# A retention layer and a snake MLP on one core: q and k of the first tiles read in rows of eight tokens, group 0 in another order, first states summed in 64x64 tiles

## The chip, the core and the metric

The kernel runs on one core of a Trainium2 chip. The metric is the device time of one execution in microseconds; the lower the better. Five engines work side by side, each through a queue of its own that it takes in order: TensorE (PE in the profile, its weight loads PEld), VectorE (DVE), ScalarE (ACT), GpSimd (POOL) and SyncE (SP). In this kernel POOL's queue also issues nearly all reads from memory.

## The reference, cut to what matters

```python
# q, k, v: float32 [4 batches, 8 heads, 768 tokens, 64]
gamma = 1.0 - 2.0 ** (-5.0 - np.arange(H))
for t in range(S):
    state = gamma * state + einsum('bhd,bhe->bhde', k[:, :, t], v[:, :, t])
    y[:, :, t] = einsum('bhd,bhde->bhe', q[:, :, t], state) / sqrt(64)
x = y.transpose(0, 2, 1, 3).reshape(3072, 512)
h = x @ w_in                        # w_in 512 x 2048
s = np.sin(alpha * h)
g = h + s * s / (alpha + 1e-9)
out = g @ w_out                     # w_out 2048 x 512, out 3072 x 512 float32
```

## The kernel before

**Tiles.** Tokens are cut into chunks of 128: six in each of the four batches, 24 in all. `order` takes the first chunk of each batch first (called e0 to e3), then the others batch by batch; P is the same list, so P4 is the fifth tile. The tiles form groups of 4, 2, 2, 2, 2, 2, 2, 2, 2 and 4. The MLP runs group by group.

**Attention of a tile.** The recurrence is worked out chunk by chunk: q and k are transposed (`half_T` for e0 to e3, `stage_T` for P4 to P7, a transposing DMA from the SP queue in `turn` for the rest), scores are multiplied out (`stage_A`, later `scores`), masked and weighted with powers of gamma on VectorE into aT, and multiplied with v (`stage_M`, later `round_of` and `mix`). A first chunk has no earlier state. For all later ones a `burst` runs on TensorE: the state times q (`inter`), the next tile's scores, the mix with v, and the update of the state (`sums`, or inside `round_of`). VectorE then writes x (`leave`, run as "exit"), adds the state (`keep`), and another engine rounds it (`hand`). v is scaled with powers of gamma (`scale_v`) before it enters a state.

**The states of first chunks.** When a burst ends one batch, its state sums are those of the next batch's first chunk (`now` is then not `old`). They are eight matmuls with all 128 tokens as the contracted dimension, behind the mix.

**The MLP.** A `Slot` multiplies x with 128 columns of w_in for each f that it covers, takes the sine on ScalarE, squares it on ScalarE ("A") or VectorE ("D"), and on VectorE adds it to h (`add`, L496). `ff_out` multiplies one f of one tile with w_out (128x512, called a piece here), 16 pieces for a tile. From group 1 on, `phase` interleaves the slots of a group with the pieces of the group before it and with the bursts at fixed places.

**Group 0** is written out by hand. While reads arrive, TensorE runs fillers (`idle_work`). The first three tiles' x is made as their reads land, slots 0 to 3 (called a, b, c, d) run on those three tiles alone, e3 is worked in between, its columns of slots 0 to 3 are made up in one further slot (t here), and slots 4 to 15 run on all four tiles. The pieces of tiles 0, 1 and in part 2 follow the slots; 13 of the 26 pieces left for tiles 2 and 3 (`fill`) run before phase 1.

**Memory.** `load_chunk` reads one chunk of q, k or v through POOL's queue and turns float32 into bf16: token by token, so 256 bytes are read and 128 written at a time, 1024 packets for 128 KB. Weights come in pieces of 256 and 512 KB. q and k of e0 come through SP as float32. Eight counters serve POOL's reads in turn, so a read waits until the eighth read before it has landed.

**PSUM.** There are four single banks (tag "mm"), and two pairs ("two", "pa").

Of the kernel before, what the change touches and what calls it, by code (L numbers as in the profile page):

```python
# [16 lines left out]
def kernel(  # L17
# [32 lines left out]
    sizes = [4]+[2]*8+[4]  # L50
# [34 lines left out]

    def load_chunk(j, names="qkv"):
        for name, src in (("q", q), ("k", k), ("v", v)):
            if name not in names:
                continue
            if name == "v":  # L90
                t = big.tile([128, H, D], BF16, name="vr", tag="vr", bufs=11)
            else:
                if ("qk", j) not in raw:
                    raw["qk", j] = big.tile([128, 2, H, D], BF16, name="qkr", tag="qkr", bufs=9)
                t = raw["qk", j][:, "qk".index(name)]
# [67 lines left out]
    tok = consts.tile([128, NCH, 2], F32, name="tok")  # L163
    for b in range(2):
        nc.gpsimd.iota(tok[64 * b:64 * b + 64], pattern=[[C, NCH], [64, 2]], channel_multiplier=1, base=0,
                       allow_small_or_imprecise_dtypes=True)
    load_chunk(order[3], "qk")
    for h in range(2):
        load_w_out(0, h)
# [19 lines left out]
    for h in range(H):  # L189
        nc.scalar.activation(out=dec[:, h % 2, h // 2, :], in_=tio, func=ACTF.Exp, scale=lng[h], bias=back[:, h:h + 1])  # L190
# [16 lines left out]

    def later_tables():
        for b in range(2):
            for p in range(NP):  # L210
                nc.vector.memset(lgq[64 * b:64 * b + 64, p:p + 1], lng[head(b, p // 2, p % 2)])
# [32 lines left out]
    def half_T(j, i, eng, bank=None):  # L244

        if i == 0:
            st["qkT", j] = work.tile([128, 2 * NP, 128], BF16, name="qkT", tag="qkT", bufs=6)
        pt = psum.tile([128, NP, 128], BF16, name="pt", tag="mm", bufs=4) if bank is None else bank.rearrange("i (p t) -> i p t", p=NP)
        for p in range(NP):
            nc.tensor.transpose(pt[:, p, :], raw["qk"[i], j][:, 2 * p:2 * p + 2, :].rearrange("p h d -> p (h d)"), ident)  # L250
        o = st["qkT", j][:, i * NP:(i + 1) * NP, :]
        if eng is nc.scalar:
# [23 lines left out]
    def stage_A(j):  # L276
        qkT = st["qkT", j]
        pa = psum.tile([128, 2, NP, 128], F32, name="pa", tag="pa")
        for p in range(NP):
# [4 lines left out]
        aT = work.tile([128, 2, NP, 128], BF16, name="aT", tag="aT", bufs=2)  # L284
        m = dec.rearrange("p e n t -> p (e n) t") if j % NCH == 0 else mask_bc
        nc.vector.tensor_mul(aT.rearrange("p e n t -> p (e n) t"), pa.rearrange("p e n t -> p (e n) t"), m)
        st["aT", j] = aT
# [18 lines left out]
    def stage_M(j, bank):  # L306
# [3 lines left out]
        for p in range(NP):  # L310
            for e in range(2):
                nc.tensor.matmul(py[half(e), p, :], vs[:, 2 * p + e, :], aT[:, e, p, :],
                                 start=(p == 0), stop=True, skip_group_check=True)
        nc.scalar.copy(x_of(j), py)
# [49 lines left out]
    def sums(now, to, lo):  # L364

        ks, vs = raw["k", now], raw["v", now]
        for f in range(2 if wide(now) else 1):
            for b, m, e in heads:
                h = head(b, m, e)
                nc.tensor.matmul(to[b][half(e), lo + 64 * m:lo + 64 + 64 * m],  # L370
                                 ks[half(b), f, 2 * m + e, :] if wide(now) else ks[:, h, :],
                                 vs[half(b), f, 2 * m + e, :] if wide(now) else vs[:, h, :],
                                 start=False, stop=True, skip_group_check=True)
# [436 lines left out]
```

## Time and profile before

| | |
|---|---|
| median of 3 runs | 210.59 us (210.5 to 211.37) |
| the profiled execution | 210.93 us, its span 209.1 us |
| instructions | 5702 |
| PE busy, matmul instructions | 199.3 us, 2327 |
| DVE, ACT busy | 151.9 us each |
| POOL busy, issuing of reads among it | 116.5 us |
| TensorE clock granted | 1.00 throughout |
| queue of POOL's reads | 79248 packets, 13.38 MB |
| chain that ended last | PE 77%, DMA 13%, POOL 6% |

The profile is of one execution. In the timeline the columns are start and duration in us, engine, line, operation, output and inputs, shapes, count; in brackets the idle time before it and what ended it. In the table of windows each engine's busy time is followed by the granted clock, the DMA share and GB/s. In the groups, the two numbers behind the first bar are busy us in all and mean ns of one.

### The profile page before, as it was taken

Reading aid. Unit: us, or ns where it says so; the run is one execution under the profiler, and the core shown is the slowest. Engines: PE = TensorE matmul, PEld = TensorE weight load, DVE = VectorE, ACT = ScalarE, POOL = GpSimd, SP = SyncE. Lnnn points to the kernel's source line nnn. Section 1 sums busy time; section 2 is a strip of 40 time slices with the busy share of each in tenths; the row PEclk is TensorE's granted clock in tenths of the full one; section 3 lists DMA queues with packets and bytes.
Section 4 is the critical chain, followed back from the end, with each engine's and each line's share of the span. In section 5 each row is a group of like instructions: output and inputs, shape, how many; then the busy total and the mean of one; then the engine's idle time right before and its main releaser. Section 6 shows DMA issues by size and latency. Waiting matters only on the chain.

```text
span 209.1 us, 5702 instructions
## 1 busy us (share of the span) xinstructions
PE 199.3 (95%) x2327; PEld 123.6 (59%) x2354; DVE 151.9 (73%) x310; ACT 151.9 (73%) x309; POOL 116.5 (56%) x157
## 2 busy tenths in 40 slices
PE   7898999999999999999999999999999999999994
PEld 2444544457776766766666766766767654444453
DVE  4788788877989968768868768867788965656220
ACT  7777687557998787787787787786785779999001
POOL 8999948599999999999599911002022200000000
PEclk9999999999999999999999999999999999999999
DMA  9999999999999999999999995412412101010212
GB/s 130 149 170 194 202 200 184 151 161 198 161 126 142 79 167 183 182 100 180 143 173 159 145 176 54 103 57 47 102 54 52 50 5 50 2 50 3 100 50 100
DMA packets 102026, 24.76 MB, mean 118 GB/s; under 512 B 93024, under 2 KB 99056, under 8 KB 102000
## 3 DMA queue, kind: packets, MB, share of 16 engines
q0 software_dynamic: 79248, 13.38, 87.9%
q1 hardware_dynamic: 22608, 10.96, 26.0%
q8 instruction: 18, 0.29, 0.6%
q14 instruction: 8, 0.07, 0.1%
q10 hardware_dynamic: 144, 0.07, 0.1%
HBM read 27.27 MB, written 6.29 MB: 160 GB/s over the span
## 4 chain that ended last, share of the span: by engine, by line
PE 77%; DMA 13%; POOL 6%; issue 2%; DVE 0%; POOLq 0%; DVEq 0%
PE po L506 34%; PE ph L481 33%; DMA qkr<-in_k_dram 5%; DMA w_out<-in_moe_w_out_dram 5%; DMA w_in<-in_moe_w_in_dram 3%; PE py L336 2%; POOL qg L229 2%; PE poh L531 2%; POOL qkr L100 2%; PE py L386 1%; POOL vr L100 1%; POOL w_in L131 1%; PE pa L346 1%; PE py L395 1%; PE pt L264 1%
## 5 line engine op out<-in xcount | busy, mean ns | idle before, releaser
L496 DVE SCALAR_TENSOR_TENSOR gT<-s,rec_alpha,ph 128x256 bf16<-128x256 f32 (+3 forms) x164 | 79.9, 523 | 32.8 <-ACT s L489 32.5
L481 PE MATMUL ph<-xT,w_in 128*128 128x256 bf16 (+3 forms) x652 | 98.1, 290 | 0.3
L484 ACT ACTIVATE s<-ph,alpha_sb 128x256 f32<-128x256 f32 (+3 forms) x164 | 76.2, 507 | 30.3 <-PE ph L481 30.2
L506 PE MATMUL po<-w_out,gT 128*128 128x512 bf16 x346 | 91.3, 379 | 3.1 <-issue 2.7
L481 PEld LDWEIGHTS <-w_in 128*128 128x128 bf16 x656 | 63.3, 98 | 33.8 <-issue 1.1
L489 ACT ACTIVATE s<-s 128x512 f32<-128x512 f32 (+1 forms) x91 | 57.0, 627 | 2.9
L506 PEld LDWEIGHTS <-gT 128*128 128x128 bf16 x368 | 33.9, 98 | 29.5
L452 POOL CAST s_q<-s_f 128x256 bf16<-128x256 f32 x5 | 2.0, 397 | 35.0 <-DVE s_f L448 18.0
L518 DVE COPY o_sb<-po 128x512 f32<-128x512 f32 x20 | 13.8, 691 | 9.8 <-PE po L506 9.8
L120 POOL DMA_DIRECT2D qk_seq<-in_q_dram x24 | 17.0, 766 | 2.7 <-DMA v_seq<-in_v_dram 2.6
L120 POOL DMA_DIRECT2D qk_seq<-in_k_dram x24 | 16.8, 716 | 0.8 <-issue 0.4
L120 POOL DMA_DIRECT2D v_seq<-in_v_dram x24 | 16.9, 765 | 0.0
L156 POOL TENSOR_TENSOR v_seq<-v_seq,kgq 128x512 bf16<-128x512 bf16 x13 | 13.5, 1057 | 4.6 <-DMA v_seq<-in_v_dram 4.6
L433 DVE TENSOR_TENSOR xT<-py,qg 128x512 bf16<-128x512 f32 x19 | 13.0, 685 | 0.8 <-PE py L402 0.8
L361 DVE TENSOR_TENSOR aTw<-pa,maskq 128x768 bf16<-128x768 f32 x13 | 12.4, 954 | 0.0
L100 POOL DMA_DIRECT2D vr<-in_v_dram x11 | 10.2, 927 | 1.2 <-DMA w_in<-in_moe_w_in_dram 1.1
L551 PE MATMUL spare<-warm 128*128 128x512 bf16 x24 | 8.4, 480 | 1.2 <-DVE warm L176 1.2
L535 ACT COPY o_sb<-poh 128x256 f32<-128x256 f32 (+1 forms) x2 | 0.6, 320 | 11.7 <-PE poh L531 11.2
L349 DVE TENSOR_TENSOR aT<-pa,mask 128x1024 bf16<-128x1024 f32 x7 | 8.5, 1218 | 0.0
L452 ACT CAST s_q<-s_f 128x256 bf16<-128x256 f32 x14 | 5.5, 393 | 3.1 <-DVE s_f L446 2.7
L100 POOL DMA_DIRECT2D qkr<-in_k_dram x7 | 6.3, 896 | 1.7 <-DMA w_out<-in_moe_w_out_dram 1.7
L100 POOL DMA_DIRECT2D qkr<-in_q_dram x7 | 6.4, 910 | 0.9 <-DMA w_in<-in_moe_w_in_dram 0.9
(99 smaller groups left out, 160.8 us busy)
## 6 DMA issues: line engine op xcount, KB each, us to landing
out_dram<-o_sb SPq DMA_DIRECT2D x23, 256.0 KB, 2.6
w_in<-in_moe_w_in_dram POOLq DMA_DIRECT2D x6, 256.0 KB, 10.3
w_out<-in_moe_w_out_dram POOLq DMA_DIRECT2D x3, 512.0 KB, 11.2
vr<-in_v_dram POOLq DMA_DIRECT2D x11, 128.0 KB, 5.5
qk_seq<-in_q_dram POOLq DMA_DIRECT2D x16, 80.0 KB, 7.1
qk_seq<-in_k_dram POOLq DMA_DIRECT2D x16, 80.0 KB, 5.2
v_seq<-in_v_dram POOLq DMA_DIRECT2D x16, 80.0 KB, 5.3
qkr<-in_q_dram POOLq DMA_DIRECT2D x7, 128.0 KB, 6.8
```

Source lines behind the costliest of these rows:

```text
L100: nc.gpsimd.dma_start(out=t, in_=chunk_of(src, j))
L120: nc.gpsimd.dma_start(out=o, in_=src[bt, head(b, m, e), cs[0] * C:, :].rearrange("(f i) d -> i f d", i=64))
L156: eng.tensor_mul(t, t, by[:, j % NCH, :, None].to_broadcast([128, H, D]))
L349: return {"mask": lambda: nc.vector.tensor_mul(aT.rearrange("p e n t -> p (e n) t"), pa.rearrange("p e (n t) -> p (e n) t", n=NP), mask_bc)}
L361: return {"mask": lambda: nc.vector.tensor_mul(aT, pa[:, :, 0:384].rearrange("p e (m t) -> p e m t", m=2), maskq[:, None, None, :].to_broa ...
L433: nc.vector.tensor_mul(o, st["pyw", old][:, :, 0:256].rearrange("p b (m t) -> p b m t", m=2), by)
L481: nc.tensor.matmul(self.ph[:, m, :], w_in[:, i, f * 128:(f + 1) * 128], xT[g][:, i, self.lo:self.hi], start=(m == 0 and i == 0), stop=(i = ...
L484: nc.scalar.activation(out=self.s[:, m, :], in_=self.ph[:, m, :], func=ACTF.Sin, scale=alpha_sb[:, f:f + 1])
L489: nc.scalar.activation(out=self.s, in_=self.s, func=ACTF.Square)
L496: nc.vector.scalar_tensor_tensor(gT[self.g][:, f, self.lo:self.hi], self.s[:, m, :], rec_alpha[:, f:f + 1], self.ph[:, m, :], op0=ALU.mult ...
L506: nc.tensor.matmul(po[g, ts], gT[g][:, f, ts * C:(ts + 1) * C], w_out[:, f, :], start=(f == 0), stop=(f == FF - 1))
L518: nc.vector.tensor_copy(o_sb, po[g, ts])
```

## The change

- **Rows.** q of e1, e2, e3 and k of e2, e3 are read as 128 rows (16 for each head) of eight tokens: 2 KB read and 1 KB written at a time. Partition p then holds eight neighbouring tokens of one head. `half_T` turns such a tile with sixteen 64x64 transposes, and the copy out of PSUM puts the tokens back in order. k of e1 goes to a tile of its own; the tag of the other q and k has seven buffers instead of nine.
- **k back.** The states of e2 and e3 need k by token. `back_k` turns it back from its transposed form, in two bursts each (old = P10, P11 and P15, P16), with a copy on VectorE.
- **First states.** `sums` works in 64x64 tiles for both cases; the two halves of the tokens go to columns of their own, which `keep` adds up. It now runs ahead of the scores. In the last burst half of the mix runs ahead of the wait for `inter`.
- **Group 0** has another order: the reads, the fillers, the masks apart from the scores (`mask_A`), x of e1 and e2 copied by VectorE, the transposes of e3 ahead of slot a, first tables on other engines (`tok` on VectorE), `later_mask` in phase 2, and the slots, squares, sums and pieces listed one by one. The transposes of e0 and e1 read one head each (64 columns).

```diff
+    def rows_of(t, j):
+        b, c = divmod(j, NCH)
+        return t[b, :, c * C:(c + 1) * C, :].rearrange("h (i f) d -> h i (f d)", f=8)
+    def load_rows(j, name):
+        src = q if name == "q" else k
+        t = raw[name, j] = big.tile([128, 8, D], BF16, name=f"{name}f", tag=f"{name}f", bufs=3 if name == "q" else 2)
+        nc.gpsimd.dma_start(out=t.rearrange("p f d -> p (f d)"), in_=rows_of(src, j))
+    def by_rows(j, name):
+        return name == "q" and j in order[1:4] or name == "k" and j in order[2:4]
...
-    load_chunk(0, "v")
-    load_chunk(order[1])
-    load_chunk(order[2])
-    for h in range(2):
-        load_w_in(0, h)
...
-    load_chunk(order[3], "qk")
-    for h in range(2):
-        load_w_out(0, h)
+    load_chunk(order[1], "k")
+    load_chunk(order[3], "k")
+    load_chunk(order[1], "q")
+    load_chunk(order[2], "k")
+    load_chunk(order[2], "q")
+    load_chunk(order[1], "v")
+    load_chunk(order[0], "v")
+    load_w_in(0, 0)
+    load_chunk(order[2], "v")
+    load_chunk(order[3], "q")
+    load_w_out(0, 0)
+    load_w_in(0, 1)
+    load_w_out(0, 1)
     load_chunk(order[3], "v")
     load_w_in(1)
     load_w_out(1)
...
+        if by_rows(j, "qk"[i]):
+            for f in range(8):
+                for x in range(2):
+                    nc.tensor.transpose(pt.rearrange("i p t -> i (p t)")[half(x), 64 * f:64 * f + 64],
+                                        raw["qk"[i], j][half(x), f, :], ident[half(x), half(x)])
+            o = o.rearrange("d m (i f) -> d m i f", f=8)
+            pt = pt.rearrange("d p t -> d (p t)").rearrange("d (f m i) -> d m i f", f=8, m=NP)
...
+    def back_k(j, x):
+        if x == 0:
+            raw["k", j] = big.tile([128, 2, NP, D], BF16, name="kn", tag="kf", bufs=2)
+        pt = psum.tile([128, NP, D], BF16, name="pt", tag="mm", bufs=4)
+        for m in range(NP):
+            for f in range(2):
+                nc.tensor.transpose(pt[half(f), m, :], st["kT", j][half(x), m, half(f)], ident[half(x), half(x)])
+        nc.vector.tensor_copy(raw["k", j][:, x], pt)
...
     def sums(now, to, lo):
-        for f in range(2 if wide(now) else 1):
+        for r in range(2):
             for b, m, e in heads:
...
+                    h, f = head(b, m, e), b ^ r
+                    bank, at, vh = f, lo + 128 * r, vs[half(f), h, :]
+                    kh = ks[half(f), h // NP, h % NP, :] if now in order[2:4] else ks[half(f), h, :]
+                last = nc.tensor.matmul(to[bank][half(e), at + 64 * m:at + 64 * m + 64], kh, vh,
+                                        start=False, stop=True, skip_group_check=True)
...
     def burst(old, new, first=None, apart=False):
...
+        elif now is not None and now is not old:
+            last = sums(now, st["py", old], 256)
         more = scores(new) if new is not None else {}
+        if old in P[10:12] + P[15:17]:
+            back_k(e2 if old in P[10:12] else e3, (P.index(old) - 10) % 5)
...
         if wide(old):
-            mix(old)
-            if now is not None and now is not old:
-                sums(now, py, 256)
+            mix(old, rest)
...
+    # group 0, around the first three tiles and slot a
+    stage_A(e0)
+    half_T(e1, 0, nc.scalar)
+    half_T(e1, 1, nc.scalar)
+    idle_work(4)
+    later_tables()
+    stage_A(e1)
+    mask_A(e0)
+    mask_A(e1)
+    half_T(e2, 0, nc.vector)
+    half_T(e2, 1, nc.scalar)
+    stage_M(e1, front[:, 0], nc.vector)
+    stage_A(e2)
+    stage_M(e0, front[:, 0])
+    mask_A(e2)
...
+    stage_M(e2, front[:, 0], nc.vector)
+    half_T(e3, 0, nc.vector)
+    half_T(e3, 1, nc.scalar)
+    slot("a", 0, 0, n3, 1, "mm")
+    scale_v(e2, nc.vector)
+    slot("b", 1, 0, n3, 1, "mm")
+    stage_A(e3)
+    sl["b"].sq("A")
+    sl["a"].sq("D")
+    slot("c", 2, 0, n3, 1, "mm")
+    slot("d", 3, 0, n3, 1, "mm")
+    sl["a"].add()
...
+    mask_A(e3)
+    sl["c"].add()
+    stage_M(e3, pye(), nc.vector)
+    pairs(2)
+    scale_v(e3, nc.vector)
+    ff_out(0, 2, 2)
+    scale_v(e0, nc.vector)
+    scale_v(e1, nc.vector)
+    slot("t", 0, n3, n4, 4, "pa")
+    sl["t"].sq("A")
+    slot("4", 4, 0, n4, 1, "mm")
+    sl["d"].add()
```

`pairs(f)` is the piece f of tiles 0 and 1. `slot(name, ...)` makes a `Slot` under a name.

More of the change, by code (lines that the diff above doesn't have):

```diff
@@ L639 @@
     P = order
[L640 to L650 removed]
+    n2, n3, n4 = 2 * C, 3 * C, 4 * C
+    e0, e1, e2, e3 = order[:B]
     outs = out_pieces(0, (2, 3))[6:]
+    sl, more = {}, {}
     def fill(n):
@@ L695, with slot, pairs @@
-    scale_v(P[4], nc.gpsimd)
-    m4 = scores(P[4])["mask"]
-    F((0, 1), (13,))
-    fill(1)
-    stage_T(P[5], nc.scalar, "mm")
-    a.add()
-    m4()
-    fill(4)
-    scale_v(P[5], nc.vector)
-    fresh = burst(P[4], P[5], apart=True)
-    run(fresh, "keep", "hand", "mask")
-    F((0, 1), (14,))
-    F((0, 1), (15,))
-    run(fresh, "exit")
+    def slot(name, f, lo, hi, nf=1, tag="mm"):
+        sl[name] = Slot(0, f, (lo, hi), nf, tag)
+    def pairs(f):
+        if f == 0:
+            both = psum.tile([128, 2, d_model], F32, name="po", tag="two")
+            po[0, 0], po[0, 1] = both[:, 0], both[:, 1]
+        for t in range(2):
+            ff_out(0, t, f)
@@ L711 @@
+    fill(1)
+    pairs(14)
+    upto(burst(P[4], P[5], apart=True))
     load_chunk(P[7])
```

347 lines of the change are left out of this document (206 added, 141 removed).

## The prediction

> **What bounds the kernel now.** I read the page's busy shares first, then the chain that ended last, then the timeline from 0 to 50 us, the windows with their DMA rates, the groups by form, and one stretch of the late phases.
>
> ```profile
> PE 199.3 (95%) x2327; PEld 123.6 (59%) x2354; DVE 151.9 (73%) x310; ACT 151.9 (73%) x309; POOL 116.5 (56%) x157
> ```
>
> ```profile
> 8.40 7.19 DMA w_in<-in_moe_w_in_dram
> ...
> 21.51 9.47 DMA w_out<-in_moe_w_out_dram
> ...
> 31.26 9.52 DMA qkr<-in_k_dram
> 40.83 0.41 PE pt L264 x8
> ```
>
> TensorE bounds the span. Until 40.83 us the chain runs through transfers, after that through matmuls alone. So the change can save time in two ways: group 0 starts or flows earlier, or the later phases lose matmul time.
>
> ```profile
> 14.75 1.46 PE L481 MATMUL ph<-xT,w_in 128*128 128x384 bf16 x8
> ...
> 21.83 1.05 PE L481 MATMUL ph<-xT,w_in 128*128 128x128 bf16 x16
> ...
> 23.26 1.72 PEld L481 LDWEIGHTS <-w_in 128*128 128x128 bf16 x9 [0.22 <-DMA w_in<-in_moe_w_in_dram]
> ...
> 23.36 1.89 PE L481 MATMUL ph<-xT,w_in 128*128 128x512 bf16 x8
> ...
> 47.60 1.03 PE L481 MATMUL ph<-xT,w_in 128*128 128x256 bf16 x8
> ```
>
> These are the marks of the front: slot a at 14.75, the fourth tile's slot t at 21.83, slot 4 at 23.36 just behind its weights (second quarter of w_in), and phase 1 at 47.60. From slot 4 to phase 1 TensorE has 12 slots of 0.87 us, 39 output pieces of 0.217, three transposes of 0.57, first states 0.32, scores 0.42 and two bursts of about 1.0: 23.3 of the 24.24 us. There is little idle time to win there; the gain has to come from slot 4 starting earlier.
>
> ```profile
> 5.00:10.00 5.00, 4.18 (x49) 2.58 (x49) 3.50 (x14) 3.56 (x12) 4.93 (x9) 1.00 2.40 149
> ...
> 20.00:25.00 5.00, 4.42 (x39) 2.53 (x39) 3.58 (x7) 2.30 (x6) 5.00 (x7) 1.00 1.29 203
> ```
>
> The last column is GB/s written. From 5 to 10 us chunk reads in 128-byte packets run at 149; from 20 to 25 us weights in packets of 512 B and 1 KB run at 203.
>
> **Row reads.** One chunk (128 KB written) costs 0.88 us of transfer at 149 GB/s and 0.65 at 203. A row read writes 1 KB packets like those of w_out, so I take 203. The same set of reads stands ahead of w_in's second quarter in both kernels, and five are now rows: 5 x 0.23 = 1.15 us, so those weights arrive at 22.1 instead of 23.26. Bounds: nothing (rows pay like chunks), and 2 us (rows near the 250 to 290 GB/s of the first float32 reads). Issue stays about 0.7 to 0.9 us each on POOL (w_out 0.75, chunks 0.91). Each POOL read waits for the eighth before it, and those landed long before.
>
> **The first three tiles.** A chunk landed 4.8 us after its issue began. The fifth read (q of e2) then lands at 9.4 to 9.9 and the ninth (v of e2) at 13.0 to 13.7. VectorE's order is longer than before: both casts and the masking of dec end at 6.97. Four small additions for tok (rows of this kind: 0.06 to 0.50 each, I take 0.25, near L186's 0.23) and the tables (0.43) end at 8.4; mask of e0 1.22, 9.6; scores of e1 0.4 behind it; mask of e1, 11.4; the copy of e2's q; the copy of x of e1 0.69; mask of e2 1.22; reciprocals 0.72; the copy of x of e2 0.69.
>
> The row copies read PSUM with a step of 64 elements, which no row here shows.
>
> ```profile
> L518 DVE COPY o_sb<-po 128x512 f32<-128x512 f32 x20 | 13.8, 691 | 9.8 <-PE po L506 9.8
> ...
> L255 DVE COPY qkT<-pt 128x512 bf16<-128x512 bf16 x3 | 1.3, 421 | 1.3 <-PE pt L250 1.2
> ```
>
> 512 adjacent bf16 take 0.42 us, 512 float32 take 0.69. I take 0.69, since nothing is adjacent any more, and keep 0.42 to 1.2 (the price of 1024 elements) as bounds. The Trainium skill (VectorE: DVE Perf Modes, "Mode 2×_1P — pack two bf16 into one 32-bit read") asks for a step of one for the double pace; by it the copy falls back to 0.69, and without it the two copies on this path would give 0.5 us back. The chain goes 11.4, 12.1, 12.8, 14.0, 14.7, 15.4: slot a at 15.45, 0.7 later than before, but with the transposes of e3 (0.8 us in all) already done on TensorE. ScalarE's Sin table load (1.28) now follows x of e0 and ends at 15.9; its copy of e3's k ends at 16.5, and the first sine starts then (before: 15.65).
>
> **From slot a to slot 4.** TensorE: a and b 0.65 each, scores of e3 0.4, c and d, six pieces of 0.217: 19.8. VectorE from 16.1: scaling of e2's v 0.68, square of a 0.52 (0.69 x 384/512) behind its sine at 17.1, sums a and b 0.61 each, mask of e3 1.22: 20.05. Then stage M of e3 to 20.5, c's sum, the copy of x to 21.4, three pieces under it, slot t 0.9: slot 4 at 22.35, behind its weights at 22.1. That is 1.01 before the old mark, but three pieces (0.65) that were done by then are still owed. One entry into 64-wide tiles is saved, because the scores of P4 now follow the transposes of P5 directly (the weight loader sat 0.42 idle at such entries; I take 0.3). Phase 1 then starts at 22.35 + 24.24 + 0.65 - 0.3 = 46.94: **0.7 earlier**. Three scalings (0.68 to 1.12 each) stand ahead of d's sum, which frees slot 6's bank and feeds the pieces of f 3; TensorE reaches them at 24.1, VectorE at 23.5 to 24.8, so up to 0.7 can be lost.
>
> **The later phases.** The sums for the first state of batches 2 and 3 were eight 128x64 matmuls behind the mix; now they are sixteen 64x64 ahead of the scores.
>
> ```profile
> 93.25 1.04 PE L481 MATMUL ph<-xT,w_in 128*128 128x256 bf16 x8
> ...
> 94.53 0.30 PE L370 MATMUL pa<-v_seq,qk_seq 64*64 64x64 bf16 x16
> ...
> 95.16 0.81 PE L506 MATMUL po<-w_out,gT 128*128 128x512 bf16 x3 [0.16 <-issue]
> ...
> 101.01 1.04 PE L481 MATMUL ph<-xT,w_in 128*128 128x256 bf16 x8
> ...
> 103.22 0.81 PE L506 MATMUL po<-w_out,gT 128*128 128x512 bf16 x3 [0.16 <-issue]
> ```
>
> An ordinary burst takes 1.91 us from its slot to the next piece, this one 2.21, though the ordinary one already holds sixteen 64x64 sums. So two such bursts save 0.3 each, 0.6. The Trainium skill (TensorEngine Tiling (Array Packing), "Key Properties") says that a change of tiling mode drains the array; the gap of 0.3 agrees with it.
>
> The last burst waited 0.23 for its first products; half of the mix now fills that: 0.2. Against this, back_k adds four times eight transposes. Sixteen 64x64 on four tiles took 0.30; these use two, so I take 0.12 each, bounded by 0.1 and 0.28: 0.5 in all. Their copies (0.42 or less), two more sums of 0.28 in keep, and the mask's 0.78 moved to phase 2 fall on VectorE, which is busy 16.46 of the 20 us from 60 on and 15.29 of the next 20; the slots between bursts hide them, and if they do not, they cost 0.4. Fewer qkr buffers cost nothing: seven chunks use the tag. Net: **-0.3** (from -0.7 to +0.8).
>
> **Sum.** The profiled execution took 210.93 us, 1.8 more than its span of 209.1. 210.93 - 0.7 - 0.3 = 209.9. The median of the runs, 210.59, lies 0.34 under that execution, so I forecast 209.6.
>
> **The rivals.**
> 1. *The weights become the only gate.* If tok costs 0.06 a piece and the row copies 0.42, VectorE's chain ends 1.3 us sooner, and rows at 250 GB/s bring w_in at 21.5; slot 4 starts at 21.6 and the end is 0.8 below my sum: 208.8. For: each is a bound from a row. Against: both must hold. 0.2.
> 2. *Rows do not pay.* If a 128-packet read costs what a chunk does, w_in comes at 23.3, slot 4 waits for it, and the three owed pieces eat the saved entry: front +0.3, sum 210.6. For: rows at 203 are inferred from other transfers. 0.22.
> 3. *Slower: VectorE gates group 0.* VectorE has work without a gap from slot a to about 33 us in the new order. If the row copies take 1.2, the masks, x of e2, e3's copy and the three scalings all move; each microsecond passes to slot 6, and phase 1 with it. It decides from 1.0 late at d's sum; at 2.0 late the front is +1.3 and the sum 211.6, with the unhidden 0.4 it is 212.0. For: TensorE and VectorE meet within 0.3 us at d, at slot 10 and at the pieces of f 6. Against: ScalarE holds the other three row copies. 0.18.
>
> **How the numbers follow.** My forecast has 0.40, with its own range 209.0 to 210.2. A measurement of this kernel tells about 0.5% (1.05 us) from no change: faster means under 209.54, slower over 211.64. Half of my case, 0.2, and rival 1 are faster: 0.40; the other half and rival 2 are the same: 0.42; rival 3 is slower: 0.18. The range from 208.4 to 211.8 takes in the rivals' middles and leaves out the far ends.
>
> **What would show it.** Right: w_in's second quarter used at about 22.1; slot a at 15.0 to 15.8; slot 4 near 22.4; phase 1 near 46.9; the burst into a new batch no longer than an ordinary one; row copies at 0.69. Wrong: TensorE waiting for VectorE at slot 6 or 10, slot 4 waiting for w_in past 23, or the four bursts with back_k longer by over 0.3.

## The result, and the profile after

The changed kernel took 211.86 us in the median of 15 runs (210.15 to 213.48); the kernel before 210.5 in the runs beside it (209.87 to 211.37). The ratio is **1.0045, 95% interval 1.0023 to 1.0067**: 0.95 us slower. Ratios leave out executions that lie more than 1.5% above the shortest of their kernel: one of the changed kernel's 15 and one of e17_three's 13, and of twelve each three of e2_table, two of e5_recip and of e6_both, four of e11_after4 and of e13_mask. The medians of all runs lie 1.36 us apart. The profiled execution of the changed kernel is one of its shortest: 210.62 us, span 208.8, which is 0.31 us less than the profiled one of before. So the traces alone show a gain where the runs show a loss, and both have to be explained. The traced execution of before is itself on the long side (210.93 beside a median of 210.5). e8_tail (below) has the same reads and the same group 0; in its trace TensorE loads the weights of w_in's second quarter from 22.67 and not 23.26, and phase 1 starts at 47.02 and not 47.60:

```profile
22.67 2.56 PEld L496 LDWEIGHTS <-w_in 128*128 128x128 bf16 x13 [0.24 <-DMA w_in<-in_moe_w_in_dram]
...
47.02 1.03 PE L496 MATMUL ph<-xT,w_in 128*128 128x256 bf16 x8
```

The page of the changed kernel first, then the chain that ended last, up to slot a (start, duration, what):

```profile
PE 202.4 (97%) x2473; PEld 124.2 (59%) x2473; DVE 156.1 (75%) x322; ACT 151.5 (73%) x309; POOL 115.0 (55%) x155
```

```profile
3.09 4.83 DMA qf<-in_q_dram
...
7.97 0.44 PE pr L283 x16
...
8.91 0.97 PE spare L628 x4
...
10.26 1.23 DVE aT L345
...
12.75 1.22 DVE aT L345
13.97 1.55 DVE rec_alpha L728
...
15.71 0.64 DVE xT L374
...
16.39 0.82 PE ph L558 x4
```

Before, the chain went through reads until 40.83 us. Now one read is left in it, q of e1. From there on it runs through TensorE and VectorE without a pause: transposes of e1, four fillers, VectorE's masks, the reciprocals of alpha, x of e2, slot a at 16.39. L728 adds 1e-9 to alpha, 16 columns, and takes longer here than a mask of 1024.

The timeline at phase 1, the row of the windows from 5 to 10 us, GpSimd's issue that waits for the second quarter of w_in, and a row copy:

```profile
47.07 1.03 PE L558 MATMUL ph<-xT,w_in 128*128 128x256 bf16 x8
```

```profile
5.00:10.00 5.00, 3.86 (x62) 1.90 (x56) 3.90 (x16) 3.36 (x10) 5.00 (x7) 1.00 1.63 163
```

```profile
21.93 0.87 POOL L119 DMA_DIRECT2D qkr<-in_q_dram  x1 [1.81 <-DMA w_in<-in_moe_w_in_dram]
```

```profile
11.40 0.68 DVE L294 COPY qkT<-pr 128x512 bf16<-128x512 bf16 x1
```

Reads run at 163 GB/s where they ran at 149; w_in's second quarter has landed by 21.9 and slot 4 (22.94) no longer waits for it; the row copy takes 0.68. Phase 1 is 0.53 earlier than in the trace of before, and not earlier than in that of e8_tail. From phase 1 to the end it takes 161.7 us, 0.2 more than before.

### The profile page after: what moved, and what is told of

Same layout as the page of the kernel before. It is cut to its first block, busy times and chain, and to the rows that moved or that the text cites. A ratio compares the mean times of both kernels' runs of the same rounds, so it can differ in the third digit from the quotient of the medians.

```text
span 208.8 us, 5979 instructions
## 1 busy us (share of the span) xinstructions
PE 202.4 (97%) x2473; PEld 124.2 (59%) x2473; DVE 156.1 (75%) x322; ACT 151.5 (73%) x309; POOL 115.0 (55%) x155
## 4 chain that ended last, share of the span: by engine, by line
PE 90%; DVE 4%; DMA 2%; POOL 1%; issue 1%; ACT 0%; POOLq 0%; DVEq 0%; ACTq 0%
PE ph L558 39%; PE po L583 39%; DMA qf<-in_q_dram 2%; PE py L396 2%; DVE aT L345 2%; PE poh L608 2%; PE py L450 1%; PE pt L303 1%; PE pa L406 1%; DVE gT L573 1%; DVE rec_alpha L728 1%; PE py L459 1%; PE pa L413 1%; PE pa L435 1%; PE spare L628 1%; POOL k L119 1%
## 5 line engine op out<-in xcount | busy, mean ns | idle before, releaser
L583 PE MATMUL po<-w_out,gT 128*128 128x512 bf16 x368 | 94.8, 380 | 0.1
L119 POOL DMA_DIRECT2D vr<-in_v_dram x11 | 10.3, 944 | 0.4 <-DMA w_out<-in_moe_w_out_dram 0.3
L150 POOL DMA_DIRECT2D w_in<-in_moe_w_in_dram x7 | 5.6, 811 | 1.6 <-DMA w_out<-in_moe_w_out_dram 1.6
L396 PE MATMUL py<-qkT,s_q 64*64 64x128 bf16 x160 | 6.1, 228 | 0.0
```

What stands on the lines that cost most here:

```text
L119: nc.gpsimd.dma_start(out=t, in_=chunk_of(src, j))
L583: nc.tensor.matmul(po[g, ts], gT[g][:, f, ts * C:(ts + 1) * C], w_out[:, f, :], start=(f == 0), stop=(f == FF - 1))
```

## The experiments

Marks are the starts of slot a, slot 4 and phase 1. "After" is the changed kernel. Each run of ratios has the kernel before beside it on its chip. Theories: **A**, TensorE's clock falls to half in the front because there are fewer early fillers; **B**, VectorE's reciprocals wait for a table product of GpSimd's; **C**, an earlier slot a is not handed on; **D**, the chain from e1's q to slot a is rigid; **E**, maskq in phase 2 costs time; **F**, GpSimd's later products take back what the front wins. In the expectations of e1 to e4, C still means that the reads vary, and in e7_again D means that they come late.

### The clock, the reads, the table product

**e1_fill**: after, with more fillers early on.

```diff
     half_T(e0, 0, nc.scalar)
-    idle_work(1)
+    idle_work(4)
     half_T(e0, 1, nc.scalar)
-    idle_work(2)
+    idle_work(3)
...
     stage_A(e0)
+    idle_work(2)
```

> The changed kernel with six more fillers on TensorE between 5 and 8 us (three between the transposes of e0's q and k, one behind them, two behind its scores). Theory A (the clock): the changed order keeps TensorE so little occupied in its first 8 us that in some executions it is granted half its clock for a stretch of the front; those executions are the slow ones of the 15 (granted mean 0.990 to 0.992, spans 211.4 to 211.7 against 208.4 to 209.4). Then no execution here shows a mean under 0.997, and the median falls from 211.9 to 210.9 or less. Theory B (the shared port): what varies is how long VectorE's small operations wait for GpSimd's table; then the spread from 210.2 to 213.5 and the median of 211.9 stay. Theory C (the reads vary): also unchanged.

Measured: 212.08, ratio 1.0062 (1.0039 to 1.0085). The granted clock was 1.00 in all eight executions, where three of after's 15 had 0.990 to 0.992; the time did not fall. The executions lie closer together, within 1.0 us (211.24 to 212.22) where after's spread over 3.3, which theories B and C did not expect.

**e4_few**: the kernel before, with five early fillers less.

```diff
-    idle_work(9)
+    idle_work(8)
...
-    idle_work(2)
+    idle_work(1)
...
-    idle_work(2)
     stage_A(e0)
...
-    idle_work(1)
     half_T(e1, 1, nc.vector)
```

> The kernel before with four fillers fewer in the first 8 us (8 instead of 9 at the start, 1 instead of 2 between the transposes of q and k of e0, none instead of 2 behind them, none instead of 1 between the transposes of e1). Theory A: this kernel, else unchanged, now shows executions with a granted mean of 0.990 to 0.992 and a spread of 2 us or more, with a median 0.5 to 1.5 above 210.5. Theories B and C: 210.3 to 210.6 as before, with the same spread of 1.5 us.

Measured: 210.75, ratio 1.0018 (0.9999 to 1.0037). Nine of twelve executions had a clock of 0.982 to 0.992. (The expectation says four fillers; its own list adds up to five.) A row of the windows of its trace (us, then busy time of PE, PEld, DVE, ACT, POOL, then the clock):

```profile
7.83:14.66 6.83, 6.58 (x52) 3.73 (x53) 4.52 (x15) 4.83 (x11) 6.76 (x11) 0.50 1.89 154
```

So few fillers do bring stretches at half clock, here twice 3.41 us on end, but phase 1 came only 0.43 later than in the trace of before. Theory A is real and too small: it goes with after's three executions at 211.4 to 211.7 us of span and does not explain the middle of the distribution. Nor is it the only way to such times: e13_mask (below) has four executions near 213 us at a clock of 1.00.

**e3_norows**: after with all q and k read in chunks, k contiguous, no back_k.

```diff
-        return name == "q" and j in order[1:4] or name == "k" and j in order[2:4]
+        return False
```

> The changed kernel with its order of group 0 and of the reads, but q and k read token by token as before, and so without turning k back (ten buffers for q and k). Theory C (rows make the reads vary): the spread goes and the median falls below 211. Theory A and B: the spread stays. By the sum of the prediction w_in's second quarter lands 1.15 to 1.6 us later than with rows (21.65 there), slot 4 at 23.2 to 23.4, and phase 1 starts 0.3 to 1.0 later than 47.07.

Measured: 211.4, ratio 1.0041 (1.0018 to 1.0064), like after. Rows do not cause the loss; the order of group 0 and the late phases are left. Two marks were missed. GpSimd and VectorE in the timeline:

```profile
22.50 0.87 POOL L119 DMA_DIRECT2D qkr<-in_q_dram  x1 [1.27 <-DMA w_in<-in_moe_w_in_dram]
```

```profile
13.97 0.17 DVE L726 TENSOR_SCALAR rec_alpha<-alpha_sb 128x16 f32<-128x16 f32 x1
```

Without rows w_in's second quarter has landed by 22.50, so rows are worth 0.57 there (21.93 in after) and not 1.15. And slot 4 came 0.40 earlier than in after, at 22.54, though 23.2 to 23.4 was expected: in this trace the addition to alpha took 0.17, ahead of GpSimd's product (15.57), and slot a came at 15.61. Phase 1 came at 47.13, 0.06 later than in after.

**e2_table**: after, with one GpSimd table product issued four reads later.

```diff
     load_chunk(order[4], "q")
-    decay_table(3)
     load_w_in(2, 0)
     load_w_in(2, 1)
     load_w_out(2)
     load_w_in(3, 0)
+    decay_table(3)
```

> The changed kernel with the first of GpSimd's table products (c = 3) issued four reads later, behind the read of w_in's fourth quarter, first half. In the profile of the changed kernel the 16-column addition for the reciprocals took 1.62 us and ended with GpSimd's product. Theory B: it now takes 0.5 or less, slot a starts near 15.3 instead of 16.39, slot t near 21.4, slot 4 at 22.0 to 22.4, the median falls by 0.5 to 1.0, and the spread shrinks if this wait is what varies. Theory A: slot a moves, but executions with a clock of 0.99 remain and the spread with them. Theory C: spread unchanged.

Measured: 210.97, ratio 1.0005 (0.9983 to 1.0027): most of the loss gone. VectorE and GpSimd in the timeline of after, then VectorE and slot a in that of e2_table:

```profile
13.88 1.62 DVE L728 TENSOR_SCALAR rec_alpha<-alpha_sb 128x16 f32<-128x16 f32 x1
15.54 0.25 DVE L729 RECIPROCAL rec_alpha<-rec_alpha 128x16 f32<-128x16 f32 x1
15.71 0.63 DVE L374 CAST xT<-front 128x512 bf16<-128x512 f32 x1
```

```profile
14.32 1.14 POOL L254 TENSOR_TENSOR qg<-qg,step 128x512 f32<-128x512 f32 x1
```

```profile
13.91 0.68 DVE L728 TENSOR_SCALAR rec_alpha<-alpha_sb 128x16 f32<-128x16 f32 x1
...
14.80 0.69 DVE L374 CAST xT<-front 128x512 bf16<-128x512 f32 x1
```

```profile
15.57 1.47 PE L558 MATMUL ph<-xT,w_in 128*128 128x384 bf16 x8
```

In after the small addition ends at 15.50, just behind GpSimd's product (14.32 + 1.14 = 15.46). Without the product it takes 0.68, x of e2 starts 0.91 earlier, and slot a comes at 15.57. Theory B holds: the wait exists, and the loss shrinks with it. How it gets into the median these traces don't show: the two traced executions are equally long (210.56 and 210.62), since of 0.82 won at slot a 0.39 is left at phase 1, and the stretch with maskq, discussed below, takes about as much back.

### The reciprocals and the order of reads

**e5_recip**: after with the reciprocals moved off the path.

```diff
-    nc.vector.tensor_scalar_add(rec_alpha, alpha_sb, 1e-9)
-    nc.vector.reciprocal(rec_alpha, rec_alpha)
...
     half_T(e3, 0, nc.vector)
+    nc.vector.tensor_scalar_add(rec_alpha, alpha_sb, 1e-9)
+    nc.vector.reciprocal(rec_alpha, rec_alpha)
```

> The changed kernel with the two small operations on rec_alpha moved on VectorE from ahead of the copy of x of e2 to behind the copy of e3's q; GpSimd's table product for c = 3 stays early. Theory B (VectorE's rec_alpha waits for GpSimd's product, 1.62 us instead of 0.47, and delays x of e2): x of e2 follows the mask directly at about 13.9, slot a starts near 14.8 instead of 16.4, phase 1 0.4 to 0.6 earlier, ratio to the kernel before 0.998 to 1.001. If the copy of x itself waits for GpSimd's product, slot a stays at 16.0 or later and the ratio at 1.004. Theory C (the work between slot a and phase 1 is bound by something else, so an earlier slot a is not handed on): slot a early, phase 1 still at 47.0 and the ratio 1.003 to 1.005.

Measured: 210.66, ratio 1.0012 (0.9986 to 1.0038), near the 0.998 to 1.001 of theory B. Its traced execution (span 212.3) is a long one, with a stretch at half clock from 9.9 to 13.3 us, and slot a at 17.88; the mark can't be compared.

**e6_both**: the edits of e2_table and e5_recip together.

> As the run before, and GpSimd's table product for c = 3 also moved behind two more weight reads. Theory B: nothing more to win than in the run before when the reciprocals are already off the path; slot a near 14.8, ratio 0.998 to 1.001. If the product costs in another way too (the reads of w_in queued behind it on GpSimd by 1.1 us), this run is another 0.3 to 0.5 us faster than the one before: 0.996 to 0.999.

Measured: 210.88, ratio 1.0025 (0.9998 to 1.0052). No more is won than by either edit alone, as it should be if both remove the same wait; the three intervals overlap. In its trace the full clock is only recorded from 10.3 us on, TensorE is late, and slot a comes at 16.67: the miss of the mark is that execution's.

**e7_again**: after once more, for its trace.

> The changed kernel once more, for a second trace. Its executions spread over 3 us, and the first trace shows one of the shortest. If this execution lies 0.5 us or more above it, the marks (slot a, slot 4, phase 1, last group) show where the time goes: theory A (the clock at half for one window in the front) puts it ahead of slot 4 with a share of half clock in the record; theory D (the reads arrive later in some executions) puts it ahead of slot a or slot 4 at full clock; if the late phases are longer, it is neither.

Measured: 211.26, span 209.5, clock 1.00. TensorE in its timeline:

```profile
8.44 0.25 PE L283 MATMUL pr<-ident,qf 64*64 64x64 bf16 x4 [0.87 <-DMA qf<-in_q_dram]
```

```profile
16.86 0.32 PE L558 MATMUL ph<-xT,w_in 128*128 128x384 bf16 x1 [0.77 <-DVE xT L374]
```

q of e1 was used 0.47 later than in the first trace (8.44 against 7.97), and slot a (16.86), slot 4 (23.42) and phase 1 (47.54) all came 0.47 or 0.48 later: 8.42 us from the one to the other in both. The other 0.2 us lie behind phase 1 (see maskq).

**e9_order**: after with e1's q read earlier.

```diff
     load_chunk(order[1], "k")
-    load_chunk(order[3], "k")
     load_chunk(order[1], "q")
...
+    load_chunk(order[3], "k")
     load_chunk(order[3], "q")
```

> The changed kernel with k of e3 read just ahead of q of e3 and no longer second, so that q of e1 is issued one read (0.64 us) earlier. In seven traces with the changed front, slot a comes 8.42 us behind the first transposes of e1's q where rec_alpha waits 1.62 us (16.39 - 7.97, and 16.86 - 8.44), and 7.5 to 7.8 where it waits less. Theory D: this chain is rigid, so whatever delays e1's q (its arrival, a late clock, fillers) is handed on to the end. Then e1's q is transposed near 7.3 to 7.5, VectorE's mask of e1 follows the mask of e0 with little idle time, slot a starts near 15.8, and the median falls by 0.4 to 0.8: ratio 0.999 to 1.002. Theory A (the clock alone): the ratio stays at 1.003 to 1.006, with executions at a mean clock of 0.99 as before.

Measured: 211.13, ratio 1.0029 (1.0012 to 1.0046). In its trace e1's q was ready for TensorE at 7.83, 0.14 earlier than in after and not the 0.5 or more expected. Slot a came at 15.41, 0.98 earlier, but x of e1 only 0.13 (12.01 against 12.14). VectorE and GpSimd behind it:

```profile
13.75 0.23 DVE L728 TENSOR_SCALAR rec_alpha<-alpha_sb 128x16 f32<-128x16 f32 x1
```

```profile
14.90 1.06 POOL L254 TENSOR_TENSOR qg<-qg,step 128x512 f32<-128x512 f32 x1
```

The addition to alpha was over before GpSimd's product began, so the wait of theory B fell away by itself; theory D accounts for 0.13 of the 0.98. The ratio is still a loss, here and in e3_norows, with no such wait in the trace: theory B is not the whole loss. Slot 4 came at 22.3, 0.64 earlier than in after, and phase 1 at 47.16, 0.09 later. Theory C is right for what follows: e2_table had already handed on only 0.39 of 0.80 from slot 4 to phase 1, here nothing of 0.64 is left.

**e10_all**: the edits of e6_both and e9_order.

> All three moves at once: e1's q one read earlier, GpSimd's table product for c = 3 later, the reciprocals behind the copies on VectorE. Theories B and D together: slot a near 14.5 to 14.9, then the second quarter of w_in (21.6) is next to gate slot 4; phase 1 at 46.2 to 46.7, ratio 0.995 to 0.999. If slot 4 or the pieces behind it are bound by something else, the ratio is 0.999 to 1.002.

Measured: 210.86, ratio 1.0020 (1.0002 to 1.0038), slot a 15.23, slot 4 22.27, phase 1 46.84. The better of the two expectations failed. Slot a stops at 15.2 because VectorE now waits 0.81 for TensorE ahead of x of e2: the products of e2 (0.41) start at 13.94, behind four more fillers (12.97 to 13.94).

**e11_after4** and **e12_before4**: four more fillers ahead of e1's scores, in after and in before.

```diff
-    idle_work(4)
+    idle_work(8)
     later_tables()
     stage_A(e1)
```

```diff
     grow(1)
+    idle_work(4)
     stage_A(e1)
```

> The changed kernel with four more filler matmuls on TensorE just ahead of the scores of e1 (eight in place of four, 0.87 us at full clock). Theory D: the chain from e1 to slot a has no slack, so slot a, slot 4 and phase 1 all come 0.8 to 0.9 later and the time is 0.8 us above the changed kernel's: ratio 1.007 to 1.010. If the front has slack, under 0.3 us is seen: ratio 1.004 to 1.006.

> The kernel before with the same four filler matmuls ahead of its scores of e1. Theory D: here VectorE is still masking e0 or busy when those scores are ready, and TensorE waits for reads later (q of e3, v of e3 and the second quarter of w_in between 16 and 23.4 us), so most of the 0.87 us is absorbed: slot a up to 0.6 later, slot 4 and phase 1 0 to 0.3 later, ratio 1.000 to 1.002. If the front before is as rigid, it costs 0.8: ratio 1.004.

Measured: 1.0071 (1.0043 to 1.0099) for after, 1.0027 (1.0013 to 1.0041) for before. In after's trace the chain behaves as theory D has it: e1's q at 7.82, and slot a 8.80 later. That is 8.42, and 0.87 for the fillers, less 0.48 because the addition to alpha now meets less of the product (1.14 in place of 1.62): 8.81. In the trace of before slot a is 1.12 later, but slot 4 only 0.14 and phase 1 0.07, taken up by later waits for reads. The ratios don't bear that out: the fillers cost after 0.0026 and before 0.0027. That before has slack and after none is so in these traces, and not shown for the median.

### The late phases

**e8_tail**: the kernel before with only the new sums, `keep` and last mix.

```diff
+        elif now is not None and now is not old:
+            last = sums(now, st["py", old], 256)
         more = scores(new) if new is not None else {}
...
-            if now is not None and now is not old:
-                sums(now, py, 256)
```

> The kernel before with only the change to the late bursts: the first states of batches 2 to 4 summed in sixteen 64x64 ahead of the scores, two more additions in keep, half of the last mix ahead of its wait; k stays contiguous, so no back_k. My prediction priced this at -0.8 us (0.6 for two bursts and 0.2 at the end): ratio 0.996. The trace of the changed kernel shows only about 0.09 us won at each of those bursts: ratio 0.998 to 1.000, and the burst from its slot to the next piece near 1.9 us.

Measured: 210.53, ratio 0.9998 (0.9976 to 1.0019). TensorE alone: the first-state burst of after, the slot behind that of before, and an ordinary burst of after:

```profile
100.63 1.04 PE L558 MATMUL ph<-xT,w_in 128*128 128x256 bf16 x8
...
101.73 0.29 PE L435 MATMUL py<-vr,kn 64*64 64x64 bf16 x16
...
102.00 0.20 PE L417 MATMUL pa<-qkT 64*64 64x64 bf16 x4
102.23 0.37 PE L450 MATMUL py<-aTw,v_seq 64*64 64x128 bf16 x16
...
103.40 0.38 PE L558 MATMUL ph<-xT,w_in 128*128 128x256 bf16 x2
```

```profile
103.87 0.38 PE L481 MATMUL ph<-xT,w_in 128*128 128x256 bf16 x2
```

```profile
94.11 0.20 PE L417 MATMUL pa<-qkT 64*64 64x64 bf16 x4
94.14 0.30 PE L435 MATMUL pa<-v_seq,qk_seq 64*64 64x64 bf16 x16
94.27 0.35 PE L450 MATMUL py<-aTw,v_seq 64*64 64x128 bf16 x16
```

From slot to slot that is 2.77 us (100.63 to 103.40; 100.43 to 103.20 in e8_tail); before it was 2.86 (101.01 to 103.87). So a burst wins 0.09 and the two win 0.18. (From the slot to the next piece, as the prediction measured, it is 2.21 and 1.90; but at that place the trace of before shows three pieces behind a gap of 0.16 and after's four, so a record seems to be missing there, and the two don't compare.) Between the last scores and the mix 0.23 us pass (102.00 to 102.23). In an ordinary burst the sixteen sums lie in that gap (94.11 to 94.27); here they went ahead of the scores, and the gap stayed. The last burst took 2.52 from slot to slot before (167.09 to 169.61) and 2.51 after (166.79 to 169.30): the half mix won nothing.

**e13_mask**: after with `later_mask` in the front.

```diff
     grow(2)
+    later_mask()
     mask_A(e1)
...
-    at((2, 0), lambda: later_mask())
```

> The changed kernel with one edit: maskq (two comparisons and a copy on VectorE, 0.78 to 1.3 us) is built in the front, between the masks of e0 and e1, where VectorE sat idle for 0.94 us, and no longer in phase 2. In the traces with maskq in phase 2 the time lost between 65 and 73 us was 0.03, 0.17, 0.33, 0.35, 0.35, 0.35 and 0.47 us (with the two comparisons at 0.67, 0.88, 1.03, 1.06, 1.05, 1.05 and 1.17 us). Theory E: this is the second part of the loss, and the trace shows under 0.05 lost there; slot a comes no more than 0.3 later; the ratio falls by about 0.0015 to 1.002 to 1.004. Rival: maskq delays the mask of e1 by as much as it won, ratio 1.004 to 1.005.

Measured: 210.83, ratio 1.0008 (0.9982 to 1.0033). The seven losses named above compare the times of ScalarE's sines with those of before at the two ends of that stretch; in this trace nothing is lost there, and slot a is where it was (16.38), though phase 1 came at 47.33, 0.26 later than in after's first trace. maskq in after, where 0.03 was lost, and in e9_order, where 0.47 was; then TensorE in e9_order:

```profile
62.55 0.68 DVE L243 TENSOR_SCALAR maskq<-tio,tok 64x128 bf16<-64x128 f32 x2
```

```profile
62.64 1.18 DVE L243 TENSOR_SCALAR maskq<-tio,tok 64x128 bf16<-64x128 f32 x2
```

```profile
69.71 1.03 PE L558 MATMUL ph<-xT,w_in 128*128 128x256 bf16 x8 [0.18 <-DVE o_sb L595]
```

VectorE is late from 62.6 on and catches up only when a slot waits for it. Theory E holds for the traces. That the ratio fell by 0.0037 where 0.35 us are 0.0017 lies within the two intervals; with all twelve executions the median is 210.83 beside 210.43, a ratio of 1.0019. (In the trace of e5_recip 0.59 was lost in that stretch with a maskq of 0.66, so it isn't the only thing that can go wrong there.)

**e14_all_mask** is e10_all and e13_mask together; **e15_all_nobackk** also reads k of e2 and e3 in chunks, without `back_k`:

```diff
-        return name == "q" and j in order[1:4] or name == "k" and j in order[2:4]
+        return name == "q" and j in order[1:4]
...
-        if old in P[10:12] + P[15:17]:
-            back_k(e2 if old in P[10:12] else e3, (P.index(old) - 10) % 5)
```

> All three moves in the front (q of e1 read earlier, table product later, reciprocals behind the copies) and maskq in the front as well. Theories B, D and E add up: 1.002 less 0.0015 gives a ratio of 0.999 to 1.001; the late phases lose only back_k's 0.25 us against 0.17 won at the first states. If maskq in the front takes the idle time that the chain of e1 needs, 1.001 to 1.003.

> As the run before, but k of e2 and e3 is read as chunks, contiguous, so that back_k is not needed; q of the second to fourth tile stays in rows. The two steps of 0.12 to 0.13 us that traces with back_k show near 85 and 125 us go, 0.25 us in all: 0.0012 below the run before, ratio 0.997 to 1.000, and faster than the kernel before if the front holds. If two more chunk reads delay w_in or the transposes of e2 by 0.2 us or more, the two runs come out equal.

Measured: 1.0002 (0.9981 to 1.0024) and 1.0013 (0.9994 to 1.0031); the second is not faster than the kernel before, and the two can't be told apart. e14_all_mask comes out as forecast from e10_all. From after the parts do not add up: e2_table and e13_mask alone lower its ratio by 0.0040 and 0.0037, everything together by 0.0043. The intervals are too wide to share the loss out. From phase 1 to the end it takes 161.74 us (46.72 to 208.46), e15_all_nobackk 161.34 (47.10 to 208.44): in these two traces back_k costs 0.40, not the 0.25 I had read. But with k in chunks slot 4 came at 22.68 in place of 22.1, which gives the 0.4 back. So rows for k are worth about what turning k back costs.

### Where the earlier front goes

In e14_all_mask slot 4 is 0.84 earlier than in after, and phase 1 0.35. VectorE, GpSimd and TensorE there:

```profile
31.57 1.67 DVE L568 TENSOR_TENSOR s<-s 128x512 f32<-128x512 f32 x1 [0.86 <-ACT s L561]
```

```profile
31.64 1.05 POOL L254 TENSOR_TENSOR qg<-qg,step 128x512 f32<-128x512 f32 x1
```

```profile
33.96 1.02 PE L558 MATMUL ph<-xT,w_in 128*128 128x512 bf16 x4 [0.34 <-DVE gT L573]
```

L568 squares s on VectorE; the next expectation calls it an addition. The same square takes 0.69 where it is alone. It ends 0.55 behind the end of the product. The product follows the issue of a read (30.67 to 31.62) that itself waits until another read has landed, however early TensorE and VectorE are.

**e16_table4** puts that product beside another one, earlier; **e17_three** also takes two of the four fillers away that stand ahead of e1's scores.

```diff
     decay_table(1)
+    decay_table(4)
     load_chunk(order[6], "v")
-    decay_table(4)
```

```diff
-    idle_work(4)
+    idle_work(2)
     later_tables()
     stage_A(e1)
```

> The run with all three front moves and maskq in the front, with one more edit: GpSimd's table product for c = 4 directly behind the one for c = 1, ahead of the wait for the next read. In the traces with an earlier front the addition of s on VectorE at 31.6 to 31.8 us took 1.67 (all three moves and maskq) and 1.91 us (read order alone) in place of 0.69, and ended 0.55 to 0.65 us behind the end of GpSimd's product that started at 31.64 and 32.07 us; TensorE's slot 9 then waited 0.34 and 0.57 us for VectorE. In the changed kernel the same addition starts at 32.41 and takes 0.85. Theory F: GpSimd's product is pinned by the landing of a read near 30.7, so an earlier VectorE runs into it, and up to 0.5 us of an earlier front is given back there. Then with the product gone from that place the addition takes 0.7 to 0.9, phase 1 starts 0.3 to 0.5 earlier (46.2 to 46.5 at a slot 4 of 22.1), ratio 0.998 to 1.000. Rival: slots behind it are bound by ScalarE, phase 1 stays at 24.6 us behind slot 4, ratio 1.000 to 1.002.

> As the run before, with two filler matmuls less on TensorE ahead of the scores of e1 (two in place of four, 0.43 us). If the chain from e1's q to slot a is rigid, slot a comes 0.2 to 0.4 earlier (ScalarE's copy of k ends 0.3 us ahead of the scores) and the ratio is 0.001 lower than in the run before; if the shorter filling lets the clock fall to half, executions at a mean clock of 0.99 appear and the ratio is 0.001 to 0.003 higher.

Measured: e16_table4 210.56 beside 210.77, ratio 0.9987 (0.9969 to 1.0005). VectorE and GpSimd in its timeline:

```profile
31.95 0.69 DVE L568 TENSOR_TENSOR s<-s 128x512 f32<-128x512 f32 x1 [0.86 <-ACT s L561]
```

```profile
29.62 2.06 POOL L254 TENSOR_TENSOR qg<-qg,step 128x512 f32<-128x512 f32 x2
```

The square is back at 0.69, as theory F has it. But phase 1 stayed at 46.86 behind a slot 4 at 22.17, 24.69 us. In this trace part of the time is lost earlier, where the weight loads wait for w_in; in e14_all_mask they ran from 26.63:

```profile
27.21 1.41 PEld L558 LDWEIGHTS <-w_in 128*128 128x128 bf16 x8 [0.62 <-DMA w_in<-in_moe_w_in_dram]
```

So the rival's mark came true, though not through ScalarE. That the ratio lies 0.0015 under that of e14_all_mask is within the two intervals.

**e17_three: 210.11 beside 210.77, ratio 0.9971 (0.9951 to 0.9992).** This version is 0.3% faster than the kernel before, the only one whose interval lies under 1. That the two fillers did it isn't shown: the interval overlaps that of e16_table4. One of its 13 executions shows a lower clock, and it is the traced one, 216.15 us, so the mark of slot a can't be read: e0's k came late, full clock is recorded from 10.3 us only, slot 4 came at 23.41, and the front then ran into the double product. VectorE, GpSimd and TensorE, then the windows (columns as above):

```profile
28.74 3.17 DVE L568 TENSOR_TENSOR s<-s 128x512 f32<-128x512 f32 x1
```

```profile
29.30 2.05 POOL L254 TENSOR_TENSOR qg<-qg,step 128x512 f32<-128x512 f32 x2
```

```profile
32.74 0.60 PE L583 MATMUL po<-w_out,gT 128*128 128x512 bf16 x2 [2.26 <-DVE gT L573]
```

```profile
34.21:37.62 3.41, 3.41 (x10) 1.21 (x9) 1.61 (x3) 1.21 (x2) 3.27 (x4) 0.50 1.66 189
```

A square of 0.69 took 3.17, TensorE stood still for 2.26 us, and then ran at half clock for 3.41. Slot 4 to phase 1 took 29.2 us in place of 24.7.

## Why the prediction was wrong, step by step

Forecast 209.6 (range 208.4 to 211.8, slower 0.18); measured 211.86. Two steps failed: the term for the reciprocals, and the sum made against one execution of before and carried to the median. The gains of the late bursts and the loss by maskq were mis-sized beside them. VectorE's mask of e1 in after, then the addition to alpha in before with GpSimd's issue beside it:

```profile
10.26 1.22 DVE L345 TENSOR_TENSOR aT<-pa,dec 128x1024 bf16<-128x1024 f32 x1 [0.94 <-PE pa L333]
```

```profile
13.27 0.47 DVE L590 TENSOR_SCALAR rec_alpha<-alpha_sb 128x16 f32<-128x16 f32 x1
```

```profile
12.83 0.91 POOL L100 DMA_DIRECT2D vr<-in_v_dram  x1
```

- **Rows: the mark came true, the term did not.** w_in's second quarter was forecast for 22.1 and landed by 21.9. But the sum gave rows 1.15 us, at 203 GB/s; from 5 to 10 us reads ran at 163, and e3_norows, with no rows, had those weights by 22.50: rows are worth 0.57. The rest of the distance to 23.26 is not theirs (e8_tail has 22.67 with before's own reads), so that the mark fits is in part luck. Rival 2 (rows do not pay) had 23.3 for reads without rows, which is wrong by the same trace. Row copies forecast at 0.69, measured 0.68.
- **VectorE's chain, right in its numbers but for one term.** Forecast 11.4, 12.1, 12.8, 14.0 for the ends of the mask of e1, the copy, x of e1 and the mask of e2; the trace has 11.48, 12.08, 12.83, 13.97. The first fits by luck: the mask of e0 was done at 9.32 and not 9.6, and VectorE then waited 0.94 for the scores of e1, which hang on the read of e1's q and on four fillers; the sum had no such path. Then "reciprocals 0.72" took from 13.88 to 15.71, 1.83. **This term failed.** It came from the trace of before, in which GpSimd was issuing reads at that time; the change put a product there (issued ahead of w_in's third quarter), and I followed the queue it left, not the engine it would meet. Slot a came 0.94 later than forecast (16.39 against 15.45), slot 4 0.59 (22.94 against 22.35), phase 1 0.13 (47.07 against 46.94): from slot 4 to phase 1 it took 24.13 where the sum had 24.59, so a second error hid most of the first.
- **maskq, priced at nothing.** "The slots between bursts hide them, and if they do not, they cost 0.4." The size was right, the case was not: 0.03 to 0.17 in four traces with maskq in phase 2 (the first of after among them), 0.33 to 0.47 in five.
- **back_k, right.** Forecast 0.5, measured 0.40.
- **First states and last burst, mis-sized.** Forecast 0.6 and 0.2 won, measured 0.18 and 0.01. I had taken the whole difference to an ordinary burst, without asking what filled the gap ahead of the mix there. If a change of tiling mode costs anything here, sums in 64x64 won no more than 0.09 of it a burst.
- **The sum from one execution.** The later phases came to +0.2 in the trace and not -0.3, the front to -0.53 and not -0.7: by its own trace the sum missed by 0.72 (210.62 against 209.9). The 0.7 was counted from before's phase 1 at 47.60, and e8_tail shows 47.02 for the same group 0: against that the front won nothing. I then took off 0.34 because the median of before lay that far under its trace; after's lies 1.24 over its own. This step carried an offset from one kernel to another, and 0.34 + 1.24 is the largest part of the miss.
- **Rival 3** named the right engine in the wrong place: VectorE gates group 0, but ahead of slot a and not from slot a to 33 us; the row copies did not take 1.2.

What makes after's executions spread by 3 us is shown in part: the arrival of e1's q (0.47 in two traces), GpSimd's product, maskq, half clock. Without the wait of theory B most of the loss is gone in two runs (1.0005 and 1.0012), but kernels whose traces have no such wait still lose (1.0029 and 1.0041). How much each has in the median stays open, and so does why before pays as much for four fillers.

## What to carry to other kernels

When an order is changed, look at what every other engine does at the new time, most of all at small operations on VectorE beside GpSimd's work: the old row's duration is that of the old neighbour. A removed wait for a read doesn't only win time, it puts the chain that was hidden behind it on the path, with all its variation. And a sum made against one execution should not be moved to the median by the other kernel's offset; take the spread of both into the range.

## What the runs showed of the hardware

**VectorE waits for GpSimd, by operation.** The addition to alpha (input and output in SBUF) took 0.16 to 0.68 with only issues of reads beside it (e6_both, e2_table), and 0.96, 1.14 and 1.62 where it met the product (e1_fill, e11_after4, after), each time ending 0.04 to 0.05 behind the product. The square of s (both inputs in SBUF) took 0.69 alone, and 1.67, 1.91 and 3.17 beside a product (e14_all_mask, e9_order, e17_three). An operation that reads PSUM was not lengthened: in e5_recip the mask of e2 ran from 15.09 beside a product from 15.39 and took 1.21 as ever. The Trainium skill (SBUF — State Buffer, "Who interferes with whom") says that a VectorE instruction with two SBUF inputs contends with a GpSimd instruction that reads SBUF, that a tensor_scalar can contend too, and that whoever issues first holds the shared pair of ports. The traces agree on who is hit. On the order they differ: the square's record starts 0.07 (e14_all_mask) and 0.56 us (e17_three) ahead of GpSimd's product and ends about 0.55 behind it, so by its end GpSimd went first each time; in both cases GpSimd was issuing a read when the square's record began.

**The clock in steps.** Full clock was recorded from 3.9 to 10.3 us after the start in the traces of kernels with nearly the same fillers, and stretches at half clock lasted 3.41 or 6.83 us. The Trainium skill (TensorE: Matmul & The Clock Gate, "What's actually happening") describes a window of 3.41 us that runs freely and doesn't start with the kernel; the lengths agree. One such stretch followed 2.26 us of idle time in e17_three; 3.41 us at half pace cost up to 1.7 us of work, an estimate, which is more than the wait of theory B.
